# Moving the loads of v, k and q of chunks 2 to 5 into the first-layer stretch: forgetting attention and a GELU MLP on one core

## The chip, the cores and the metric

The kernel runs on one core of a Trainium2 chip. The metric is the device time of one execution in microseconds. The times shown are of three runs of the kernel before the change; a fourth execution was taken by the hardware profiler, and every row of the trace is from that one. Engines are named as in the profile: PE is TensorE (PEld its weight loads), DVE is VectorE, ACT is ScalarE, POOL is GpSimd, SP is SyncE. L208 is line 208 of the kernel.

## The reference

Attention with a forget gate for 8 batches of 8 heads, 576 tokens and head size 64, and behind it an MLP with GELU (tanh form) on all 4608 tokens, 512 to 2048 to 512 columns. All in float32.

```python
scores = scale * np.matmul(q, k.transpose(0, 1, 3, 2))
log_f = np.log(np.clip(f, 0.0001, 1.0))
cum = np.cumsum(log_f, axis=-1)
decay = cum[:, :, :, None] - cum[:, :, None, :]
scores = np.where(causal, -1000000000.0, scores + decay)
attn = softmax(scores)            # exp of scores less the row's maximum, over their sum + 1e-9
x = np.matmul(attn, v)            # then (B, S, H, D), as 4608 rows of 512
h = x @ w_in
g = 0.5 * h * (1.0 + np.tanh(c * (h + 0.044715 * h * h * h)))
out = g @ w_out
```

## The kernel before

**Tiling.** Attention works in quads: four heads of one batch, so two quads to a batch and 16 quads (0 to 15) in all. The MLP works in nine chunks of 512 tokens. The two run interleaved: while TensorE works on the first layer of chunk c (from d_model to d_ff, L395 and, by a scheme with seven products for eight, L520 and L468), and then on its second layer (L600), attention of the following quads is worked in between. A step of the program is one chunk; it has two stretches, the *first-layer stretch* and, after it, the *attention stretch*, in which the scores, masks and products of two quads alternate with pieces of the second layer.

**The order of the work** is written out by hand. Tables of words (`FRONT`, `SECOND`, `STEADY`, `FLUSH`, `LAST`) are run from left to right. A word names an operation and its arguments, and each engine gets its instructions in the order in which the words issue them. `FRONT` fills the machine, `SECOND` is run for chunk 2, `STEADY` for chunks 3, 4 and 5, `FLUSH` for chunk 6 and `LAST` for chunk 7. In a step for chunk c, a word on a quad has 2c added to its first number, and a word on a chunk or batch has c added; words on quads past 15 are dropped. So `LK.6` in chunk 3 loads k of quad 12, and `LB.2.4` in chunk 3 loads part 4 of batch 5.

**Words that matter here.**

- `LK.i`, `LQ.i` (`load_one`, L208) load k or q of quad i into one of two buffers, `k_c` or `q_c`. The load turns float32 into bfloat16 and is issued on GpSimd's queue, so it stands in order with GpSimd's other work.
- `TK.i`, `TQ.i` (`transpose_words`, L214) transpose such a buffer on VectorE into `kT` or `qT`. They wait for the load; the next load of the same buffer (two quads on) waits for them.
- `LB.b.t` (`load_v`, L185) loads rows 128t to 128t + 127 of all heads of v of batch b into one of two buffers `v_nat`, on SyncE's queue. Five such loads make a batch, the last with 64 rows. On the same queue, in order, go the stores of the output from `o_st` (L625), each of which waits for VectorE to write `o_st`.
- `VW.i` (`make_vw`, L231) multiplies v of a quad by its weights, on GpSimd, into `vw`. It is the reader of `v_nat`. In the step of chunk c, `VW.3` reads the batch loaded one step earlier and `VW.4` the one loaded in the same step.
- `S.i.r` (L277 and L285) are the scores of quad i in three rounds on TensorE with the exponential on ScalarE, `M.i.r` (L291) their causal masks on GpSimd, `D.i` and `V.i.x` (L347) the products with the weights and with v on TensorE, closed on VectorE (L366 to L379).
- `I`, `i`, `Q`, `E` are pieces of the first layer, `F` and `f` pieces of the second (L600), `G` the sums on VectorE between them (L578 to L584), `T` and `UW` other sums on VectorE.

**Buffers.** `k_c`, `q_c`, `kT`, `qT`, `v_nat`, `vw` and `pt` have two copies each, `o_st` three. In the step of chunk c, TensorE scores quads 2c + 3 and 2c + 4; the transposes of both stand in the first-layer stretch. The kernel before loads quad 2c + 5 in that stretch, and quad 2c + 6 in the attention stretch, one whole first-layer stretch ahead of its transposes in the next step.

Of the kernel before, what the change touches and what calls it, by code (L numbers as in the profile page):

```python
# [16 lines left out]
def kernel(  # L17
# [12 lines left out]
    B, H, S, D = q.shape  # L30
# [55 lines left out]
    """  # L86

    SECOND = """
        Y F.-1.99 T.0.1 T.0.2 T.0.3 T.0.4 I.0.0 E.0.2.2 I.0.1 TK.3 E.0.2.2 LK.5 TQ.3 LQ.5 TQ.4 I.0.2 LB.2.4 E.0.2.2 I.0.3 E.0.2.1 TK.4 LB.2.2 G.0 VW.3
        I.0.6 I.0.7 G.1.1.2 X LB.2.3 F.0.13 S.3.0 LB.2.0 LB.2.1 M.3.0 f.0.9 UW.0.1 D.2 f.0.9 S.3.1 LQ.6 M.3.1 V.2.0 f.0.12 S.3.2 M.3.2 LK.6 CL.3 V.2.1  # L90
        VW.4 f.0.14 S.4.0 UW.0.2 M.4.0 D.3 f.0.10 V.3.0 UW.0.4 CL.4 UW.0.3 S.4.1 f.0.13 M.4.1 V.3.1 S.4.2 F.0.9 M.4.2 F.0.2 F.0.1
    """

    STEADY = """
        Q.0.2 Y T.0.1 T.0.2 F.-1.2 Q.0.2 i.0.2.4 T.0.4 i.0.2.4 T.0.3 Q.0.2 TQ.3 Q.0.2 F.-1.6 i.0.3.4 Q.0.2 Q.0.2 TK.3 i.0.3.4 Q.0.2 TK.4 TQ.4 LB.2.2
        LQ.5 LB.2.3 F.-1.99 I.0.6 i.0.7 LK.5 G.0 S.3.0 X LB.2.4 G.1.1.2 LB.2.0 LB.2.1 f.0.16 M.3.0 D.2 VW.3 f.0.12 S.3.1 LQ.6 M.3.1 V.2.0 f.0.13 S.3.2
        M.3.2 CL.3 LK.6 V.2.1 VW.4 f.0.15 S.4.0 D.3 f.0.10 V.3.0 M.4.0 CL.4 S.4.1 f.0.14 M.4.1 V.3.1 S.4.2 F.0.12 M.4.2
    """

    FLUSH = """  # L100
# [758 lines left out]
```

## Time and profile before

| | us |
|---|---|
| median of 3 runs | 327.96 |
| the runs | 327.79, 327.96, 330.09 |
| the profiled execution | 329.55 |
| its span | 326.2 |
| granted TensorE clock in it | 0.999 |
| PE, DVE, ACT, POOL busy | 311.6, 242.7, 212.9, 106.7 |

In the rows of the trace, a line such as `166.36 0.41 PE L347 MATMUL po<-pt,vw ... x5` is start, duration, engine, line, operation, what is written from what, shapes, and how many instructions are merged in it; in brackets stands how long the engine was idle before it and what ended that. A row of a DMA queue gives its packets, their megabytes, and the time that they took as a share of 16 DMA engines in that window. A row of a DMA issue gives the count, the KB of each and the median time from issue to landing. In the list of waits a row gives who waited for whom, the sum in us, the times, and the longest.

Loads and stores of the whole program: 32 loads of k and q with 288 KB each, 40 loads of v from SyncE, 35 stores of 256 KB from `o_st`. The DMA queues are q0 (issued by GpSimd, 15.99 MB), q1 (issued by SyncE, 16.60 MB), and q8 and q14 (instructions, 0.67 and 0.07 MB).

### The profile page before, as it was taken

Reading aid. Unit: us, or ns where it says so; the run is one execution under the profiler, and the core shown is the slowest. Engines: PE = TensorE matmul, PEld = TensorE weight load, DVE = VectorE, ACT = ScalarE, POOL = GpSimd, SP = SyncE. Lnnn points to the kernel's source line nnn. Section 1 sums busy time; section 2 is a strip of 40 time slices with the busy share of each in tenths; the row PEclk is TensorE's granted clock in tenths of the full one; section 3 lists DMA queues with packets and bytes.
Section 4 is the critical chain, followed back from the end, with each engine's and each line's share of the span. In section 5 each row is a group of like instructions: output and inputs, shape, how many; then the busy total and the mean of one; then the engine's idle time right before and its main releaser. Section 6 shows DMA issues by size and latency. Waiting matters only on the chain.

```text
span 326.2 us, 11823 instructions
## 1 busy us (share of the span) xinstructions
PE 311.6 (96%) x5342; PEld 221.7 (68%) x5342; DVE 242.7 (74%) x374; ACT 212.9 (65%) x242; POOL 106.7 (33%) x145
## 2 busy tenths in 40 slices
PE   0899999999999999999989999999999999999996
PEld 0556844454677567776768876767776786788785
DVE  4665208898989978879876997699884866497574
ACT  4486567785856877778657875967677743846510
POOL 8868416343111406400841056204610150000000
PEclk9999999999999999999999999999999999999999
DMA  7999999686023954268333743184001012010202
GB/s 130 232 146 163 196 247 220 141 163 125 31 43 97 224 107 83 63 113 168 75 72 51 182 100 65 43 179 112 26 32 65 4 38 66 4 54 8 98 32 97
DMA packets 47490, 33.41 MB, mean 102 GB/s; under 512 B 29776, under 2 KB 42192, under 8 KB 47440
## 3 DMA queue, kind: packets, MB, share of 16 engines
q0 software_dynamic: 9632, 15.99, 29.3%
q1 hardware_dynamic: 37664, 16.60, 18.7%
q8 instruction: 41, 0.67, 0.8%
q14 instruction: 9, 0.07, 0.1%
q10 hardware_dynamic: 144, 0.07, 0.1%
HBM read 36.85 MB, written 9.44 MB: 142 GB/s over the span
## 4 chain that ended last, share of the span: by engine, by line
PE 81%; DMA 6%; POOL 4%; DVE 4%; ACT 3%; issue 2%; POOLq 0%; DVEq 0%
PE ps_w L600 29%; PE ps_h L395 17%; PE po L347 9%; PE ps_q L520 8%; PE ps_s L277 8%; DMA w_out_sb<-in_moe_w_out_dram 4%; PE ps_u L468 4%; PE pso L667 4%; DMA q_c<-in_q_dram 2%; ACT pt L285 1%; ACT gT L403 1%; POOL pt L291 1%; DVE gT L582 1%; POOL v_nat L185 1%; PE cum_ps L721 1%
## 5 line engine op out<-in xcount | busy, mean ns | idle before, releaser
L285 ACT ACTIVATE pt<-ps_s 128x1024 bf16<-128x1024 f32 (+2 forms) x100 | 93.9, 991 | 41.8 <-PE ps_s L277 38.5
L291 POOL TENSOR_SCALAR_AFFINE_SELECT pt<-pt 128x512 bf16<-128x512 bf16 (+3 forms) x65 | 39.6, 620 | 96.5 <-ACT pt L285 73.7
L395 PE MATMUL ps_h<-xT,w_in_sb 128*128 128x512 bf16 (+1 forms) x320 | 66.8, 358 | 0.3 <-ACT gT L403 0.2
L395 PEld LDWEIGHTS <-w_in_sb 128*128 128x128 bf16 x320 | 31.2, 98 | 26.6 <-issue 0.6
L600 PEld LDWEIGHTS <-gT 128*32 128x32 bf16 (+1 forms) x1216 | 44.2, 97 | 5.7 <-issue 2.4
L403 ACT ACTIVATE gT<-ps_h 128x1024 bf16<-128x1024 f32 x34 | 34.6, 1018 | 18.6 <-PE ps_h L395 18.3
L600 PE MATMUL ps_w<-w_out_sb,gT 128*32 128x256 bf16 (+1 forms) x1008 | 42.8, 273 | 0.0
L277 PE MATMUL ps_s<-qT,kT 32*128 32x64 bf16 (+5 forms) x896 | 36.4, 264 | 3.6 <-DVE qT L214 3.3
L600 PEld LDWEIGHTS <-gsum 128*32 128x32 bf16 (+1 forms) x948 | 35.4, 97 | 3.7 <-issue 1.3
L231 POOL TENSOR_TENSOR vw<-v_nat,wT 128x1280 bf16<-128x1280 f32 (+1 forms) x13 | 30.1, 2313 | 13.0 <-DMA v_nat<-in_v_dram 12.7
L536 DVE TENSOR_TENSOR usnap<-ps_q,usnap 128x1024 f32<-128x1024 f32 x15 | 17.9, 1222 | 19.4 <-PE ps_q L520 13.2
L277 PEld LDWEIGHTS <-kT 32*128 32x128 bf16 x896 | 16.5, 93 | 19.6 <-issue 10.2
L600 PE MATMUL ps_w<-usum,gsum 128*32 128x256 bf16 (+1 forms) x791 | 29.8, 273 | 0.0
L617 DVE COPY snap<-ps_w 128x512 f32<-128x512 f32 x32 | 21.8, 681 | 6.6 <-PE ps_w L600 6.5
L347 PE MATMUL po<-pt,vw 128*32 128x64 bf16 (+4 forms) x624 | 22.9, 278 | 1.3 <-issue 1.3
L379 DVE TENSOR_TENSOR xT<-po,rb 128x576 bf16<-128x576 f32 x26 | 19.6, 753 | 6.0 <-PE po L347 5.5
L531 ACT ACTIVATE gT<-usnap 128x1024 bf16<-128x1024 f32 x15 | 15.8, 1054 | 12.1 <-DVE usnap L536 11.8
L214 DVE STREAM_TRANSPOSE kT<-k_c 128x576 f32<-128x576 f32 x16 | 19.5, 1247 | 3.7 <-DMA k_c<-in_k_dram 3.7
L347 PEld LDWEIGHTS <-vw 128*32 128x32 bf16 x672 | 14.6, 97 | 11.2 <-issue 4.9
L214 DVE STREAM_TRANSPOSE qT<-q_c 128x576 f32<-128x576 f32 x16 | 19.8, 1247 | 2.7 <-DMA q_c<-in_q_dram 2.6
L208 POOL DMA_DIRECT2D k_c<-in_k_dram x16 | 9.0, 562 | 33.6 <-DVE kT L214 17.2
L520 PEld LDWEIGHTS <-w_in_sb 128*128 128x128 bf16 x160 | 15.6, 98 | 2.5 <-issue 0.4
(134 smaller groups left out, 481.1 us busy)
## 6 DMA issues: line engine op xcount, KB each, us to landing
out_dram<-o_st SPq DMA_DIRECT2D x35, 256.0 KB, 2.6
k_c<-in_k_dram POOLq DMA_DIRECT2D x16, 288.0 KB, 4.7
q_c<-in_q_dram POOLq DMA_DIRECT2D x16, 288.0 KB, 4.9
v_nat<-in_v_dram SPq DMA_DIRECT2D x16, 256.0 KB, 5.4
v_nat<-in_v_dram SPq DMA_DIRECT2D x20, 128.0 KB, 4.4
v_nat<-in_v_dram POOLq DMA_DIRECT2D x8, 256.0 KB, 7.9
w_in_sb<-in_moe_w_in_dram POOLq DMA_DIRECT2D x8, 256.0 KB, 7.2
w_out_sb<-in_moe_w_out_dram POOLq DMA_DIRECT2D x4, 512.0 KB, 10.8
```

The costliest lines, as they stand in the source:

```text
L214: return nc.vector.transpose(out=dst.rearrange("p s c -> p (s c)").bitcast(FP32) .rearrange("p (t a) -> p a t", a=S // 32), in_=src.rearra ...
L231: return eng.tensor_mul(vw[i % 2][:, t0:t1], vb[:, t0:t1, h0:h0 + 4, :], wT[:, i, t0:t1, :].unsqueeze(3).to_broadcast([128, t1 - t0, 4, D]))
L277: nc.tensor.matmul(tiles[h // 2][:, h % 2, c0:c0 + nq], key_columns(i, key, h, c), qq[32 * h:32 * h + 32, q0:q0 + nq, c], start=(c == 0 an ...
L285: nc.scalar.activation(p[:, 2 * g:2 * g + 2, off:off + n], t[:, :, 0:n], AF.Exp, scale=scale)
L291: nc.gpsimd.affine_select(out=x, in_=x, compare_op=ALU.is_ge, fill=0.0, base=0, pattern=pattern, channel_multiplier=-1)
L347: nc.tensor.matmul(po[r0:r0 + w.shape[-1], 448 + q0:448 + q0 + nq], w, p[:, h, col:col + nq], start=(key in (0, "low")), stop=(key in ("lo ...
L379: nc.vector.tensor_mul(xT[:, 2 * u + x, r0 + s0:r0 + s1], po, rbs[i, part])
L395: nc.tensor.matmul(ph[:, j, n * cols:(n + 1) * cols], w_in_sb[:, dt, 128 * ft:128 * ft + 128], xT[:, dt, h0:h0 + cols], start=(dt == 0 and ...
L403: nc.scalar.activation(gelus(c, 2 * pr, 2), ph, AF.Gelu_apprx_tanh)
L520: nc.tensor.matmul(ps[:, k, HC * n:HC * n + HC], w[:, d, 128 * n:128 * n + 128], x[:, d, :], start=(first and n == 0 and d == 0), stop=(d ...
L600: nc.tensor.matmul(ps[c0:c0 + width, n, cols[0]:cols[1]], x[:, j, 128 * n + c0:128 * n + c0 + width], w[:, j, cols[0]:cols[1]], start=(fir ...
L617: copy(kept[name], ps)
```

## The change

Only the tables `SECOND` and `STEADY` change; no operation is added or left out. The five loads of v, which stood late in the first-layer stretch and at the start of the attention stretch (`LB.2.2`, `LB.2.3`, `LB.2.4`, `LB.2.0`, `LB.2.1`), stand at the front and the middle of the first-layer stretch, in rising order. The loads of k and q of the even quads (`LQ.6`, `LK.6` in the attention stretch) are taken out there; in `STEADY` they stand as `LK.4`, `LQ.4` at the front of the next step, which is the same quad. The loads of the odd quads (`LK.5`, `LQ.5`) stand directly behind the transposes that free their buffers.

```diff
     SECOND = """
-        Y F.-1.99 T.0.1 T.0.2 T.0.3 T.0.4 I.0.0 E.0.2.2 I.0.1 TK.3 E.0.2.2 LK.5 TQ.3 LQ.5 TQ.4 I.0.2 LB.2.4 E.0.2.2 I.0.3 E.0.2.1 TK.4 LB.2.2 G.0 VW.3
-        I.0.6 I.0.7 G.1.1.2 X LB.2.3 F.0.13 S.3.0 LB.2.0 LB.2.1 M.3.0 f.0.9 UW.0.1 D.2 f.0.9 S.3.1 LQ.6 M.3.1 V.2.0 f.0.12 S.3.2 M.3.2 LK.6 CL.3 V.2.1
-        VW.4 f.0.14 S.4.0 UW.0.2 M.4.0 D.3 f.0.10 V.3.0 UW.0.4 CL.4 UW.0.3 S.4.1 f.0.13 M.4.1 V.3.1 S.4.2 F.0.9 M.4.2 F.0.2 F.0.1
+        Y F.-1.99 T.0.1 T.0.2 LB.2.0 T.0.3 T.0.4 LB.2.1 I.0.0 LB.2.2 E.0.2.2 I.0.1 LB.2.3 TK.3 LK.5 LB.2.4 E.0.2.2 TQ.3 LQ.5 TQ.4 I.0.2 E.0.2.2 I.0.3
+        E.0.2.1 TK.4 G.0 VW.3 I.0.6 I.0.7 G.1.1.2 X F.0.13 S.3.0 M.3.0 f.0.9 UW.0.1 D.2 f.0.9 S.3.1 M.3.1 V.2.0 f.0.12 S.3.2 M.3.2 CL.3 V.2.1 VW.4
+        f.0.14 S.4.0 UW.0.2 M.4.0 D.3 f.0.10 V.3.0 UW.0.4 CL.4 UW.0.3 S.4.1 f.0.13 M.4.1 V.3.1 S.4.2 F.0.9 M.4.2 F.0.2 F.0.1
     """
 
     STEADY = """
-        Q.0.2 Y T.0.1 T.0.2 F.-1.2 Q.0.2 i.0.2.4 T.0.4 i.0.2.4 T.0.3 Q.0.2 TQ.3 Q.0.2 F.-1.6 i.0.3.4 Q.0.2 Q.0.2 TK.3 i.0.3.4 Q.0.2 TK.4 TQ.4 LB.2.2
-        LQ.5 LB.2.3 F.-1.99 I.0.6 i.0.7 LK.5 G.0 S.3.0 X LB.2.4 G.1.1.2 LB.2.0 LB.2.1 f.0.16 M.3.0 D.2 VW.3 f.0.12 S.3.1 LQ.6 M.3.1 V.2.0 f.0.13 S.3.2
-        M.3.2 CL.3 LK.6 V.2.1 VW.4 f.0.15 S.4.0 D.3 f.0.10 V.3.0 M.4.0 CL.4 S.4.1 f.0.14 M.4.1 V.3.1 S.4.2 F.0.12 M.4.2
+        LK.4 LQ.4 Q.0.2 Y LB.2.0 T.0.1 T.0.2 LB.2.1 F.-1.2 Q.0.2 i.0.2.4 T.0.4 LB.2.2 i.0.2.4 T.0.3 Q.0.2 TQ.3 LQ.5 Q.0.2 F.-1.6 i.0.3.4 Q.0.2 Q.0.2
+        LB.2.3 TK.3 LB.2.4 LK.5 i.0.3.4 Q.0.2 TK.4 TQ.4 F.-1.99 I.0.6 i.0.7 G.0 S.3.0 X G.1.1.2 f.0.16 M.3.0 D.2 VW.3 f.0.12 S.3.1 M.3.1 V.2.0 f.0.13
+        S.3.2 M.3.2 CL.3 V.2.1 VW.4 f.0.15 S.4.0 D.3 f.0.10 V.3.0 M.4.0 CL.4 S.4.1 f.0.14 M.4.1 V.3.1 S.4.2 F.0.12 M.4.2
     """
```

In the built programs TensorE's, VectorE's and ScalarE's instructions stand in the same order. GpSimd's differ only in the three pairs of loads (k and q of quads 10, 12 and 14), which stand behind the last masks of a step instead of among the masks of its first quad. SyncE's differ in the place of the v loads among the stores: in chunk 2 they stand behind the same stores as before, in another order among themselves; in chunks 3 to 5 three of them stand one store earlier than the first did before, and the other two behind the next store.

## The prediction

> **What bounds the kernel now.** I read the page first: span, busy times, chain.
>
> ```profile
> span 326.2 us, 11823 instructions
> PE 311.6 (96%) x5342; PEld 221.7 (68%) x5342; DVE 242.7 (74%) x374; ACT 212.9 (65%) x242; POOL 106.7 (33%) x145
> PE 81%; DMA 6%; POOL 4%; DVE 4%; ACT 3%; issue 2%; POOLq 0%; DVEq 0%
> ```
>
> TensorE is busy 96% of the span and carries 81% of the chain of waits. So a moved load is worth something only where TensorE stands still because of it. The profiled execution took 329.55 us, 3.35 more than its span; the median of the runs shown is 327.96, 1.59 below it.
>
> Next I cut the span of chunks 3, 4 and 5 into their two stretches: first layer, then attention. A stretch begins at the first matmul of that part, by the timeline of TensorE. The busy times by windows say this (columns: stretch, length, busy time with count for PE, PEld, DVE, ACT, POOL, then granted clock, DMA share, GB/s):
>
> ```profile
> 134.00:150.55 16.55, 16.55 (x120) 11.59 (x121) 12.94 (x17) 13.05 (x14) 2.35 (x4) 1.00 0.53 99
> 150.55:168.82 18.27, 17.43 (x578) 13.00 (x578) 15.85 (x25) 12.07 (x13) 10.34 (x12) 1.00 0.50 102
> 168.82:185.46 16.64, 16.64 (x154) 14.73 (x154) 11.97 (x16) 13.05 (x14) 2.35 (x4) 1.00 0.48 101
> 185.46:203.24 17.78, 17.28 (x578) 12.85 (x578) 15.11 (x24) 12.07 (x13) 10.34 (x12) 1.00 0.49 103
> 203.24:219.79 16.55, 16.55 (x120) 11.59 (x122) 12.79 (x17) 13.05 (x14) 2.35 (x4) 1.00 0.48 101
> 219.79:236.76 16.97, 16.97 (x578) 12.83 (x578) 14.89 (x24) 12.07 (x13) 9.66 (x10) 1.00 0.30 74
> ```
>
> The first-layer stretches are full: TensorE is busy all 16.55 to 16.64 us. The attention stretches do the same 578 matmuls but differ: 18.27, 17.78 and 16.97 us. Chunk 5's is the fast one, and it is the one without a k and a q load, because quad 16 does not exist (POOL x10 instead of x12, DMA share 0.30 instead of 0.50). The before kernel thus holds a sample of what the changed attention stretch would be. The excess is 18.27 - 16.97 = 1.30 us in chunk 3 and 17.78 - 16.97 = 0.81 us in chunk 4.
>
> The waits of TensorE and its timeline show most of it:
>
> ```profile
> PE po L347 <- issue: 1.3, 2, 0.8
> ```
> ```profile
> 166.36 0.41 PE L347 MATMUL po<-pt,vw 128*32 128x512 bf16 x5
> 167.61 0.65 PE L347 MATMUL po<-pt,vw 128*32 128x64 bf16 x19 [0.84 <-issue]
> 198.12 0.73 PE L347 MATMUL po<-pt,vw 128*32 128x512 bf16 x13
> 199.35 0.43 PE L347 MATMUL po<-pt,vw 128*32 128x320 bf16 x11 [0.50 <-issue]
> ```
>
> One product of 24 matmuls stops after 5, another after 13, for 0.84 and 0.50 us, with nothing to wait for that the profile shows. What can stop an engine inside a product is the lack of instructions, so I asked for the DMA packets. In chunk 3, 160.0 to 165.2, then 165.2 to 166.3:
>
> ```profile
> q0 software_dynamic: 275, 0.57, 75.9%
> ```
> ```profile
> q8 instruction: 1, 0.02, 5.4%
> ```
>
> In chunk 4, 192.0 to 197.1, then 197.1 to 200.3:
>
> ```profile
> q0 software_dynamic: 141, 0.29, 37.2%
> q1 hardware_dynamic: 272, 0.26, 15.3%
> ```
> ```profile
> q8 instruction: 1, 0.02, 1.9%
> ```
>
> In chunk 5, 228.0 to 231.4, then 231.4 to 232.6:
>
> ```profile
> q1 hardware_dynamic: 272, 0.26, 23.5%
> q8 instruction: 1, 0.02, 1.8%
> ```
> ```profile
> q8 instruction: 1, 0.02, 5.7%
> ```
>
> Queue q8 brings TensorE's instructions. In chunk 5 one of its packets starts in each stretch of about 3.4 us, with a store on q1 in flight. In chunks 3 and 4 there is none for more than 5 us while the k and q loads (q0, the GpSimd queue) are in flight, and TensorE stops 1.6 to 1.8 us after the late packet could start at the earliest (166.36 + 0.41 = 166.77 against 165.2; 198.85 against 197.1). I read this as refills held up by the k and q loads. In the first layer TensorE uses 120 to 154 matmuls in 16.6 us instead of 578 in 17, so a refill there has several times longer before it is missed.
>
> **The change part by part.** In all parts instructions and bytes are the same; only places change. Rows of GpSimd, VectorE and SyncE in chunk 3 carry this part:
>
> ```profile
> 136.10 1.23 POOL L291 TENSOR_SCALAR_AFFINE_SELECT pt<-pt 128x512 bf16<-128x512 bf16 x2 [2.14 <-ACT pt L285]
> 140.85 0.59 POOL L208 DMA_DIRECT2D q_c<-in_q_dram  x1 [3.53 <-DVE qT L214]
> 147.17 0.53 POOL L208 DMA_DIRECT2D k_c<-in_k_dram  x1 [5.73 <-DVE kT L214]
> 156.22 2.33 POOL L231 TENSOR_TENSOR vw<-v_nat,wT 128x1280 bf16<-128x1280 f32 x1
> 158.50 0.59 POOL L208 DMA_DIRECT2D q_c<-in_q_dram  x1
> 159.11 0.65 POOL L291 TENSOR_SCALAR_AFFINE_SELECT pt<-pt 128x512 bf16<-128x512 bf16 x1
> 160.80 1.23 POOL L291 TENSOR_SCALAR_AFFINE_SELECT pt<-pt 128x512 bf16<-128x512 bf16 x2 [1.04 <-ACT pt L285]
> 161.98 0.55 POOL L208 DMA_DIRECT2D k_c<-in_k_dram  x1
> 162.55 2.35 POOL L231 TENSOR_TENSOR vw<-v_nat,wT 128x1280 bf16<-128x1280 f32 x1
> ```
> ```profile
> 145.62 2.33 DVE L214 STREAM_TRANSPOSE kT<-k_c 128x576 f32<-128x576 f32 x2
> 147.79 1.24 DVE L214 STREAM_TRANSPOSE qT<-q_c 128x576 f32<-128x576 f32 x1
> ```
> ```profile
> 134.62 7.58 SPq L625 DMA_DIRECT2D out_dram<-o_st  x2
> 142.29 1.36 SPq L185 DMA_DIRECT2D v_nat<-in_v_dram  x2
> 150.01 2.05 SPq L185 DMA_DIRECT2D v_nat<-in_v_dram  x3
> ```
>
> Attention stretch, k and q loads of even quads (three pairs leave it, from chunks 2, 3 and 4). GpSimd's masks move up by 0.59 us at most (the one at 159.11 stands right behind a load); the next pair waits 1.04 us for ScalarE anyway, so that is worth nothing on TensorE. What is gained is the refill: I take the chunk 5 stretch for chunks 3 and 4, 1.30 + 0.81 = 2.11 us. Lower bound: the two gaps alone, 0.84 + 0.50 = 1.34. Upper bound: chunk 2 loses a pair too, and shows no gap; if it hides as much as chunk 3 has beside its gap (1.30 - 0.84 = 0.46), the gain is 2.57.
>
> First-layer stretch, the same three pairs. They stand behind the last two masks of the chunk before, so in chunk 3 they issue at 136.10 + 1.23 = 137.33 and 0.55 later. GpSimd then idles 3.53 and 5.73 us before its next two loads, which keep their places: issue costs nothing. Who waits is VectorE: the second kT transpose at about 146.8 (half of the two from 145.62) and qT at 147.79. The trace's busiest load time was in chunk 2, loads issued from 109.9 to 112.1, beside the worst landing of any q load:
>
> ```profile
> v_nat<-in_v_dram SPq DMA_DIRECT2D x3, 256.0 KB, 6.9
> k_c<-in_k_dram POOLq DMA_DIRECT2D x1, 288.0 KB, 5.4
> q_c<-in_q_dram POOLq DMA_DIRECT2D x1, 288.0 KB, 6.4
> ```
> ```profile
> DMA to landing us min/median/max: 3.8/4.9/12.6
> ```
>
> With 5.4 and 6.4 us, k lands at 142.7 and q at 144.3: 4.1 and 3.5 us early. With 12.6 both come late, k by 3.1 and q by 2.7 us. I take the first, since those loads stood between v loads on a full DMA, as these will; cost zero, at the other end 3.1 us in each of three chunks.
>
> v loads. In chunks 3 to 5 three of five follow the store at 134.62 and two the store before 142.29, instead of two at 142.29 and three at 150.01. Their buffer has been free since the chunk before (its last reader is such a product as the one at 156.22). Their reader in the same chunk is the product at 162.55: with 6.9 us of landing from 144, they are there by 151. Behind them on SyncE stand only stores. In chunk 2 they come behind the same two stores as before and only change order. Cost zero; that cover would be gone only with landings over 18 us.
>
> TensorE's refills in the first layer now meet more loads. By the fast stretch's 578 matmuls in 16.97 us and the first layer's 120 to 154 in 16.6, the use there is about four times slower, so the cover of a refill grows in the same measure; a delay of 2 us as in attention stays hidden. Bounds: 0 and, if one refill per chunk were missed as in chunk 3, 0.84 x 3 = 2.5 us. I take 0, as the three first-layer stretches show no gap with DMA shares of 0.48 to 0.53.
>
> Two rules of the Trainium skill speak against the gain. "Runtime: NRT & Kernel Launch", section Instruction fetch mechanics, says that the sequencer streams 16 KiB blocks on its own while it executes the current one, and that a boundary is mostly hidden. The block size agrees with the 0.02 MB of each q8 packet; that it is hidden does not fit the two gaps behind late packets. "DMA: Bandwidth & Descriptors", section Queues, rings and completion order, says that each engine takes turns between queues packet by packet, so that a load could hold a refill for one packet only; here none starts for 5 us. By either rule the sum would be 0 instead of -2.11.
>
> Sum: -2.11 (from -2.57 to -1.34). On the profiled execution 329.55 becomes 327.44; on the median 327.96 becomes 325.85. I forecast 325.9.
>
> **The rivals.** A: the gaps have another cause and stay. A refill may be late for itself, and the loads beside it chance; then the time is 327.96. Against it: both gaps follow a late packet, and the stretch without k and q has neither. It is also what the two rules above would make of it. Chance 0.09.
>
> B: the gaps belong to the profiled execution, 1.59 us slower than the median. If the timed runs refill in time, there is nothing to gain: 327.96. For it: the difference has the size of the gain. Against it: the loads stand in the same place in every run. Chance 0.09.
>
> C, slower: the moved k and q land late. VectorE then stands at the second kT transpose, with qT, the copy of the store, the sums for the second layer and the denominators queued behind it, and TensorE waits for these. It decides once a landing takes longer than 146.8 - 137.33 = 9.5 us. At 12.6 us it costs 3.1 us in each of three chunks, 9.3 in all; with the 2.11 gained, 327.96 + 9.3 - 2.1 = 335.2. For it: all four k and q loads and all v loads now share one first layer; v alone has five loads there. Against it: 5.4 and 6.4 us on a full DMA. Chance 0.12.
>
> D: more than 1% is gained, as the loads also slow VectorE in attention (15.85 us of work in chunk 3, 14.89 in chunk 5). TensorE does not wait for VectorE there, so 0.05; about 324.5.
>
> **How the numbers follow.** Forecast 0.65, and the rest as above. The range begins at 327.96 - 2.57 = 325.4, less 0.2 for the distance of the two nearest runs (327.79 and 327.96): 325.2. It ends with A and B at 327.96 plus twice that: 328.3. C and D, 0.17 together, are left out. A measurement of this kernel tells about 1% (3.3 us) from no change. Faster by more than that is D: 0.05. Slower by more is C: 0.12. The forecast, A and B lie within it: 0.83.
>
> **What would show it.** Right: attention stretches of chunks 3 and 4 near 17.0 us; no "issue" gap in a product; q8 packets there 3.4 us apart; q0 silent in attention. First-layer stretches stay at 16.6, with a DMA share well above 0.53. Wrong: an idle time of VectorE before kT or qT that ends with a k or q load (C); a gap of TensorE left in attention with q0 silent (A); a gap of TensorE by "issue" in a first layer (its refills missed after all).

## The result, and the profile after

The changed kernel took 325.14 us (median of 22 runs, 323.55 to 327.70), the kernel before, measured beside it, 327.23 us (22 runs, 325.44 to 330.09). The ratio is 0.9943 with a 95% interval of 0.9923 to 0.9962: 1.9 us less, between 1.2 and 2.5. That is clear of zero and below 1%. Ratios here and below leave out a few slow executions, the slowest of them 457.91 and 365.22 us at granted clocks of 0.66 and 0.86.

The busy times by windows of the changed kernel, cut like those of before (first-layer and attention stretch of chunks 3, 4 and 5; stretch, length, busy time with count for PE, PEld, DVE, ACT, POOL, granted clock, DMA share, GB/s):

```profile
135.44:151.99 16.55, 16.55 (x121) 11.59 (x122) 12.84 (x17) 13.05 (x14) 3.37 (x6) 1.00 0.88 177
151.99:168.96 16.97, 16.97 (x578) 12.87 (x578) 14.89 (x24) 12.07 (x13) 9.64 (x10) 1.00 0.11 35
168.96:185.59 16.63, 16.63 (x152) 14.71 (x153) 12.84 (x17) 13.04 (x14) 3.36 (x6) 1.00 0.85 176
185.59:202.57 16.98, 16.98 (x578) 12.87 (x578) 14.84 (x24) 12.07 (x13) 9.63 (x10) 1.00 0.10 34
202.57:219.12 16.55, 16.55 (x122) 11.59 (x120) 12.78 (x17) 13.04 (x14) 3.36 (x6) 1.00 0.87 176
219.12:236.10 16.98, 16.98 (x578) 12.79 (x578) 14.88 (x24) 12.07 (x13) 9.64 (x10) 1.00 0.11 36
```

All three attention stretches now last 16.97 to 16.98 us, the length that chunk 5 had before. The first-layer stretches kept theirs, although the DMA share there went from about 0.5 to 0.85 to 0.88. In the DMA packets of chunk 3's attention stretch (152 to 169) q0 is all but silent, and five packets of TensorE's instructions come, 3.4 to 4.3 us apart:

```profile
q1 hardware_dynamic: 527, 0.51, 8.9%
q8 instruction: 5, 0.08, 2.1%
q0 software_dynamic: 2, 0.00, 0.0%
```

The moved loads land in time. The issues from 138 to 149 with their time to landing, and the transposes on VectorE that wait for them:

```profile
k_c<-in_k_dram POOLq DMA_DIRECT2D x2, 288.0 KB, 5.0
q_c<-in_q_dram POOLq DMA_DIRECT2D x2, 288.0 KB, 6.5
```
```profile
147.06 2.33 DVE L214 STREAM_TRANSPOSE kT<-k_c 128x576 f32<-128x576 f32 x2
149.23 1.24 DVE L214 STREAM_TRANSPOSE qT<-q_c 128x576 f32<-128x576 f32 x1
```

No idle time stands before them: no bracket follows the rows. One "issue" gap is left among TensorE's waits, and it is not in these chunks but in the fill, at L419, about 32 us from the start:

```profile
PE ps_h L419 <- issue: 2.0, 1, 2.0
```

Chunk 2's attention stretch begins at 119.8 us in this execution and at 118.4 in that of the kernel before, so the spans differ by only 0.7 us (325.5 against 326.2). From there to the end it is 207.8 us before and 205.7 after.

### The profile page after: what moved, and what is told of

The parts are those of the page before. It is cut to its first block, busy times and chain, and to the rows that moved or that the text cites. A ratio compares the mean times of both kernels' runs of the same rounds, so it can differ in the third digit from the quotient of the medians.

```text
span 325.5 us, 11826 instructions
## 1 busy us (share of the span) xinstructions
PE 312.0 (96%) x5342; PEld 222.2 (68%) x5342; DVE 241.6 (74%) x374; ACT 212.7 (65%) x242; POOL 107.2 (33%) x145
## 4 chain that ended last, share of the span: by engine, by line
PE 91%; ACT 3%; DVE 2%; DMA 2%; issue 1%; POOL 0%; DVEq 0%; POOLq 0%
PE ps_w L600 30%; PE ps_h L395 19%; PE ps_s L277 9%; PE po L347 9%; PE ps_q L520 8%; PE ps_h L419 5%; PE pso L667 4%; PE ps_u L468 4%; DMA q_c<-in_q_dram 2%; PE po_m L333 1%; ACT pt L285 1%; PE cum_ps L721 1%; ACT gT L403 1%; DVE xT L379 1%; PE idle_ps L256 0%
## 5 line engine op out<-in xcount | busy, mean ns | idle before, releaser
L291 POOL TENSOR_SCALAR_AFFINE_SELECT pt<-pt 128x512 bf16<-128x512 bf16 (+3 forms) x65 | 40.8, 637 | 97.6 <-ACT pt L285 74.8
L395 PEld LDWEIGHTS <-w_in_sb 128*128 128x128 bf16 x320 | 31.2, 98 | 26.7 <-issue 0.6
L419 PE MATMUL ps_h<-xT,w_in_sb 128*128 128x256 bf16 x128 | 16.3, 291 | 2.0 <-issue 2.0
```

The source lines that it names most:

```text
L291: nc.gpsimd.affine_select(out=x, in_=x, compare_op=ALU.is_ge, fill=0.0, base=0, pattern=pattern, channel_multiplier=-1)
L395: nc.tensor.matmul(ph[:, j, n * cols:(n + 1) * cols], w_in_sb[:, dt, 128 * ft:128 * ft + 128], xT[:, dt, h0:h0 + cols], start=(dt == 0 and ...
L419: nc.tensor.matmul(ph[:, j // 2, QA * (j % 2):QA * (j % 2) + QA], w_in_sb[:, dt, 128 * ft:128 * ft + 128], xT[:, dt, n0:n0 + QA], start=(d ...
```

## The experiments

Below, "excess" is the length of the attention stretches of chunks 3, 4 and 5 above 16.97 us, read from the busy times by windows. It was 1.30 + 0.81 + 0.00 = 2.11 us before, and 0.02 after. The times of whole runs scatter by 3 us and more between executions of the same kernel, so that six or twelve of them resolve about 1 us. The excess is of one execution, but it holds nearly all by which the traces differ behind the fill: from the start of chunk 2's attention stretch to that of chunk 3's it is 32.15 to 32.17 us in every kernel but the two with wide matmuls, and from the end of chunk 5's to the last matmul 86.5 us in all. (Behind the last matmul, the first execution with only k and q moved and the one with v loaded again took 1.7 and 1.5 us longer than the others.) Both measures are given.

**One part alone.** Two kernels take the change apart: only k and q moved, only v moved.

```diff
 # only k and q: the kernel before, in SECOND and STEADY (there LK.6 stood behind CL.3)
-... S.3.1 LQ.6 M.3.1 ... M.3.2 LK.6 CL.3 ...
+... S.3.1 M.3.1 ... M.3.2 CL.3 ...
 # and at the front of STEADY
-        Q.0.2 Y T.0.1 T.0.2 F.-1.2 ...
+        LK.4 LQ.4 Q.0.2 Y T.0.1 T.0.2 F.-1.2 ...
```

> The kernel before with only the three pairs of k and q loads (quads 10, 12, 14) moved to the front of the next step; the v loads stay where they were. Theory (the k and q loads in flight hold up TensorE's instruction packets): the whole gain, 2.1 us below the kernel before (ratio about 0.994); attention stretches of chunks 3 and 4 at 17.0 us, no issue gap in a product. Rival (v loads, or DMA traffic as a whole, hold the packets): the v loads that still run into the attention stretch keep a part of the loss; less than half of the gain, ratio 0.997 or above, and gaps of 0.2 us or more remain in chunk 3 or 4.

```diff
 # only v: the changed kernel, with LQ.6 and LK.6 back in SECOND and STEADY
-        LK.4 LQ.4 Q.0.2 Y LB.2.0 T.0.1 ...
+        Q.0.2 Y LB.2.0 T.0.1 ...
-... S.3.1 M.3.1 ... S.3.2 M.3.2 CL.3 ...
+... S.3.1 LQ.6 M.3.1 ... S.3.2 M.3.2 CL.3 LK.6 ...
 # (in SECOND: M.3.2 LK.6 CL.3)
```

> The changed kernel with the three pairs of k and q loads put back into the attention stretch; only the v loads are moved. Theory: no gain, ratio 0.999 to 1.001; issue gaps of about 0.5 to 0.9 us in the products of chunks 3 and 4, stretches of 17.8 to 18.3 us. Rival (v loads or traffic as a whole): at least half of the gain, ratio 0.997 or below, gaps shorter than 0.3 us.

With only k and q moved the ratio to the kernel before was 0.9935 (0.990 to 0.997), the excess 0.56 + 0.20 + 0.00 = 0.76 us. With only v moved it was 0.9933 (0.9901 to 0.9964), the excess 0.26 + 1.41 + 0.00 = 1.67 us. So neither expectation held as a whole: by the trace most of the loss goes with k and q but a third stays, and by the runs the two halves could not be told apart. The timeline of TensorE with only v moved shows a product stopped after 13 of 24 matmuls, the one that stopped there in the kernel before:

```profile
195.60 0.73 PE L347 MATMUL po<-pt,vw 128*32 128x512 bf16 x13
197.44 0.43 PE L347 MATMUL po<-pt,vw 128*32 128x320 bf16 x11 [1.11 <-issue]
```

With only k and q moved TensorE stops elsewhere, in the second layer near the start of chunk 3's attention stretch (which begins at 148.91), where v loads are in flight. Up to 151.5 no packet of q8 starts; in the changed kernel the first comes 1.2 us into the stretch. The gap, and the packets from 148.91 to 151.5:

```profile
153.72 0.29 PE L600 MATMUL ps_w<-w_out_sb,gT 128*32 128x256 bf16 x3 [0.28 <-issue]
```
```profile
q1 hardware_dynamic: 1303, 0.52, 75.5%
q0 software_dynamic: 16, 0.02, 3.7%
```

**Loads that nobody reads.** The changed kernel, with k and q loaded once more in attention:

```diff
-... S.3.1 M.3.1 V.2.0 f.0.13 S.3.2 M.3.2 CL.3 V.2.1 ...
+... S.3.1 LQ.4 M.3.1 V.2.0 f.0.13 S.3.2 M.3.2 CL.3 LK.4 V.2.1 ...
```

> The changed kernel, and in the attention stretches of chunks 3, 4 and 5 the k and q of the quad just transposed are loaded once more, at the places where the pairs stood before; nobody reads them. Theory: the loss comes back, and in chunk 5 too, which never had it: stretches of 17.5 to 18.3 us in all three, issue gaps within products in at least two of them, 2 to 3.5 us above the changed kernel. Rival (the loss lay in the order of the loads that are waited for, not in the traffic): no gap, as nobody waits for these loads, and the time of the changed kernel within 0.5 us.

Ratio 0.9954 (0.9926 to 0.9983), the highest of the four kernels measured together, though still below the kernel before; excess 0.30 + 1.37 + 0.01 = 1.68 us. In the trace the loss comes back although nothing waits for these loads, and the gap stands after the same 13 matmuls:

```profile
196.49 0.73 PE L347 MATMUL po<-pt,vw 128*32 128x512 bf16 x13
198.27 0.43 PE L347 MATMUL po<-pt,vw 128*32 128x320 bf16 x11 [1.05 <-issue]
```

But chunk 5 stayed at 16.98, with k and q in flight. The expectation failed there: such loads in the stretch are not enough. In the packets of its stretch (223.6 to 235.7) three of q8 came, none of them late enough to be missed:

```profile
q0 software_dynamic: 288, 0.59, 32.7%
q1 hardware_dynamic: 272, 0.26, 6.6%
q8 instruction: 3, 0.05, 1.9%
```

The one that came while k and q were under way started in a lull between the two. From 230.25 to 230.85, and from there to 231.05:

```profile
q0 software_dynamic: 8, 0.01, 7.1%
```
```profile
q8 instruction: 1, 0.02, 41.2%
```

**Small loads at the same places**, 64 of the 1152 columns of each row:

```diff
+    def load_some(src, dst, i):
+        b, h0 = i // QPB, 4 * (i % QPB)
+        return nc.gpsimd.dma_start(
+            out=dst[i % 2].rearrange("p a d -> p (a d)")[:, 0:D],
+            in_=src[b, h0:h0 + 4].rearrange("h (p a) d -> (h p) (a d)", p=32)[:, 0:D])
...
-... S.3.1 M.3.1 V.2.0 f.0.13 S.3.2 M.3.2 CL.3 V.2.1 ...
+... S.3.1 SQ.4 M.3.1 V.2.0 f.0.13 S.3.2 M.3.2 CL.3 SK.4 V.2.1 ...
```

> The changed kernel with small loads at the places where the k and q loads stood in attention in chunks 3, 4 and 5: the same 128 rows, but 64 of 1152 columns, read by nobody. GpSimd's queue is occupied as before, the traffic is a twentieth. Theory (traffic of k and q in flight holds the packets): no gap, stretches at 17.0 us, time of the changed kernel within 0.5 us. Rival (the issue on GpSimd among the masks, not the traffic): stretches of 17.5 us or more and 1 us or more lost.

Ratio 0.9918 (0.9886 to 0.995), stretches 16.97, 16.98 and 16.98. GpSimd issues as many instructions among the masks as before (x12), and nothing is lost:

```profile
149.09:166.06 16.97, 16.97 (x578) 12.88 (x578) 15.11 (x24) 12.07 (x13) 10.32 (x12) 1.00 0.15 38
```

So it is the bytes in flight, not the issue on GpSimd's queue.

**The same with v**, from SyncE's queue:

```diff
-... f.0.12 S.3.1 M.3.1 V.2.0 ...
+... f.0.12 S.3.1 LB.1.0 LB.1.1 LB.1.2 LB.1.3 LB.1.4 M.3.1 V.2.0 ...
```

> The changed kernel, and in the attention stretches of chunks 3, 4 and 5 the five v loads of the batch just read are issued once more on SyncE behind the second round of scores of the first quad; nobody reads them. They bring 1.1 MB, about as much DMA time as a pair of k and q. Theory (it is the loads of GpSimd's queue that hold the packets): no gap, stretches at 17.0 us, time of the changed kernel within 0.5 us. Rival (any traffic of that size holds them): gaps and 2 to 3.5 us, as with k and q loaded again.

The expectation failed in the trace. The runs were the fastest of the four kernels measured together (0.9914, 0.9884 to 0.9945), but the trace has gaps of 0.63 us in chunk 5 and 0.29 us behind chunk 4's stretch: stretches 16.98, 17.12 and 17.89 (excess 1.08 us), and the first layer of chunk 5 at 17.00 instead of 16.55. TensorE's timeline, and the packets from 228.5 to 230.0, where a packet of q8 at last starts:

```profile
230.19 1.48 PE L600 MATMUL ps_w<-usum,gsum 128*32 128x256 bf16 x45
232.30 0.51 PE L600 MATMUL ps_w<-usum,gsum 128*32 128x256 bf16 x11 [0.63 <-issue]
```
```profile
q1 hardware_dynamic: 1388, 0.35, 118.3%
q8 instruction: 1, 0.02, 5.3%
```

From 224.7 to 229.5 there was none. So v loads can hold TensorE's packets too.

**Fewer instructions.** The second-layer matmuls of attention 128 columns wide instead of four times 32, in the kernel before and in the changed one (in `STEADY`, and alike in `SECOND`):

```diff
-... f.0.16 M.3.0 D.2 VW.3 f.0.12 S.3.1 ... f.0.13 ... f.0.15 ... f.0.10 ... f.0.14 ...
+... F.0.16 M.3.0 D.2 VW.3 F.0.12 S.3.1 ... F.0.13 ... F.0.15 ... F.0.10 ... F.0.14 ...
```

> The kernel before with the second-layer matmuls of the attention stretches of chunks 2 to 5 issued 128 columns wide instead of four times 32: the same products, about a quarter of the instructions in them. The loads stay as before. Theory (the gaps are late instruction packets, missed only because attention uses instructions fast): packets come about half as often, no issue gap, although k and q are in flight; stretches of chunks 3, 4 and 5 equal within 0.2 us. Rival (the loads slow TensorE otherwise, by its reads or writes): chunks 3 and 4 stay 0.5 to 1.3 us longer than chunk 5.

> The changed kernel with the second-layer matmuls of the attention stretches of chunks 2 to 5 issued 128 columns wide. Theory: with rare packets the place of the loads does not matter; equal to the kernel before with the same wide matmuls, within 0.5 us. Rival: still 1.5 us or more faster than that. What wide matmuls do to the time by themselves is open: from 2 us slower, if the changes of shape between them and the attention matmuls cost, to 1 us faster.

The three stretches of the kernel before, wide:

```profile
149.60:167.34 17.74, 17.74 (x338) 11.89 (x338) 14.97 (x24) 12.07 (x13) 10.32 (x12) 1.00 0.50 101
183.97:201.70 17.73, 17.73 (x338) 11.88 (x338) 14.92 (x24) 12.07 (x13) 10.32 (x12) 1.00 0.51 104
218.25:235.99 17.74, 17.74 (x338) 11.89 (x338) 14.80 (x24) 12.07 (x13) 9.64 (x10) 1.00 0.27 70
```

The loads are where they were (DMA share 0.50, 0.51, 0.27), and the stretches are equal within 0.01 us, with no gap. In the first of them two packets of q8 come instead of five:

```profile
q8 instruction: 2, 0.03, 0.7%
```

Over the whole program q8 brings 34 packets instead of 41 for 8827 matmuls and weight loads instead of 10684, about 260 to a packet both times: it follows TensorE's instructions.

The changed kernel, wide, has 17.73, 17.74 and 17.74. The ratios to the kernel before are 0.9985 (0.9956 to 1.0014) and 0.9998 (0.9972 to 1.0024): with about half as many packets in attention the place of the loads is worth nothing that the runs show. Nor is it that no packet came late: in the kernel before, wide, the third packet of chunk 4's stretch starts 15.2 us into it and the first of chunk 5's 3.7 us, in the changed kernel, wide, 14.0 and 2.3 us. These delays left no gap. The wide matmuls themselves cost 0.77 us in each stretch (17.74 against 16.97), so they are no better way.

**A late landing**, the price of rival C:

```diff
-        LK.4 LQ.4 Q.0.2 Y LB.2.0 ...
+        Q.0.2 Y LB.2.0 ...
-        LB.2.3 TK.3 LB.2.4 LK.5 i.0.3.4 Q.0.2 TK.4 TQ.4 ...
+        LB.2.3 TK.3 LB.2.4 LK.5 LK.4 LQ.4 i.0.3.4 Q.0.2 TK.4 TQ.4 ...
```

> The changed kernel with the k and q loads of quads 10, 12, 14 put behind the k load of the odd quad, the last load of GpSimd's queue in the first-layer stretch, so that they issue some 10 us later and land after VectorE comes to their transposes. It prices the slower rival of the prediction. Theory (a landing after the transposes costs TensorE what VectorE stands, less a little slack): VectorE idles 4 to 7 us before the second kT transpose in each of three chunks, TensorE loses 3 to 6 us in each, 9 to 18 us in all. Rival (VectorE has enough slack there): less than 1 us in a chunk, 3 us in all.

356.47 us, a ratio of 1.0862 (1.082 to 1.0904). VectorE stood as long as expected, 5.8 us, but TensorE lost more than the 3 to 6 us: 10.1 us in chunk 3, and 31.0 us in the three attention stretches instead of 9 to 18. VectorE's idle time, TensorE's two waits, and the granted clock behind them (window, then PE, PEld, DVE, ACT, POOL, clock):

```profile
151.36 1.26 DVE L214 STREAM_TRANSPOSE kT<-k_c 128x576 f32<-128x576 f32 x1 [5.79 <-DMA k_c<-in_k_dram]
```
```profile
154.60 1.49 PE L600 MATMUL ps_w<-w_out_sb,gT 128*32 128x256 bf16 x48 [2.11 <-DVE o_st L622]
162.55 1.53 PE L347 MATMUL po<-pt,vw 128*32 128x512 bf16 x24 [5.88 <-DVE den L366]
```
```profile
149.25:176.27 27.02, 19.02 (x578) 14.26 (x578) 20.70 (x28) 12.07 (x13) 10.08 (x10) 0.87 0.19 44
163.00:168.00 5.00, 5.00 (x124) 3.72 (x120) 3.48 (x6) 0.72 (x1) 0.00 (x0) 0.67 0.17 56
```

TensorE waits 2.11 us for the copy that frees a bank and 5.88 us for the denominators, both queued on VectorE behind the transposes. That is 8.0 of the 10.1 us. The other 2 us are longer matmuls: the mean clock of 0.67 is one of 0.50 up to 166.25, granted from 159.4 on, in the middle of the wait, and 3.7 us of it fall on matmuls.

**Again, measured together:** the kernel before, the changed one and the two halves.

> The kernel before once more, for a second profiled execution. Excess means the length of the attention stretches of chunks 3, 4 and 5 above 16.97 us, summed; it was 2.11 us. Theory now (any DMA traffic in attention can hold TensorE's instruction packets, and the gaps fall where a packet comes due while loads are in flight): they come again, an excess of 1.2 to 3 us. Rival (they belonged to that one execution): below 0.5 us. Time: equal to the kernel before.

> The changed kernel once more. Theory: excess below 0.1 us again, as only stores are in flight in attention. Rival (the clean stretches were one execution's luck): 0.5 us or more. Time: 1.5 to 2.5 us below the kernel before, in the same call as the two kernels that do one part alone.

> Only the k and q loads moved, once more; its excess was 0.56 + 0.20 + 0.00 = 0.76 us. Theory now: the v loads at the start of attention hold packets too, so an excess of 0.3 to 1.2 us again, and less gain than the whole change. Rival (k and q alone matter): below 0.2 us.

> Only the v loads moved, once more; its excess was 0.26 + 1.41 + 0.00 = 1.67 us, though its timed runs were as fast as those of the other half. Theory now: the k and q loads hold packets here, excess 0.8 to 2.2 us, and the timed gain is the smaller of the two halves, 0.0 to 1.3 us. Rival (the v loads carry the gain): excess below 0.5 us and a timed gain of 1.5 us or more.

| | ratio to before | excess, chunks 3, 4, 5 | excess in the first execution |
|---|---|---|---|
| before, again | 0.9998 (0.9965 to 1.003) | 1.01 + 0.60 + 0.11 = 1.72 | 2.11 |
| changed, again | 0.9887 (0.9844 to 0.993) | 0.00 + 0.01 + 0.00 = 0.01 | 0.02 |
| only k and q | 0.9955 (0.9922 to 0.9989) | 0.53 + 0.15 + 0.00 = 0.68 | 0.76 |
| only v | 0.9964 (0.9935 to 0.9994) | 0.97 + 1.13 + 0.00 = 2.10 | 1.67 |

The loss is no accident of one execution. In the kernel before, a product of chunk 3 stops again after 5 of its 24 matmuls, as in the first execution, only shorter (0.58 us instead of 0.84):

```profile
165.34 0.41 PE L347 MATMUL po<-pt,vw 128*32 128x512 bf16 x5
166.33 0.65 PE L347 MATMUL po<-pt,vw 128*32 128x64 bf16 x19 [0.58 <-issue]
```

Moving only k and q leaves 0.7 us, of which 0.5 us is the first part of chunk 3's stretch (5.01 us instead of 4.48), where v loads are in flight. Moving only v leaves the whole excess. Its timed gain of 0.4% (0.1 to 0.7%, and 0.7% the first time) has no counterpart in the two traces: from the start of chunk 2's attention stretch to the end they take 207.4 and 207.8 us, the kernel before 207.8 and 207.4. So this gain lies ahead of that stretch or outside the span, or comes of the scatter, and it stays open; k and q loaded again raise the same question. That the loss goes mostly with k and q rests on the traces, not on the times. The changed kernel gained more here than the first time and than expected (0.9887, some 3.7 us, against 0.9943; the intervals overlap by a little); its excess says 0.5 to 0.6%, and I take the comparison with 22 runs on each side.

**Packet by packet.** Over all these traces the gap follows the packet. In each of the eleven "issue" gaps of 0.25 us or more in these attention stretches a packet of q8 started 2.2 to 2.7 us before TensorE went on. In chunk 4's stretch the fourth packet starts 9.6 to 9.8 us after the stretch began in the changed kernel (both executions) and with small loads: excess 0.01 us. It starts at 10.6 with v loaded again and with only k and q moved, second execution (0.15), at 11.0 in the first execution of that (0.20), at 11.5 and 11.7 in the kernel before (0.60 and 0.81), and at 12.0 to 12.3 with only v moved and with k and q loaded again (1.13 to 1.41). Most of the first 1 us of delay is covered; beyond that the loss grows with the delay.

## Why the prediction was right, point by point

- **Forecast and term.** 325.9 us against 325.14, and a gain of 2.11 against 1.9 (1.2 to 2.5) by the runs and 2.09 by the excess of the first executions (2.11 - 0.02); 1.71 in the second (1.72 - 0.01). Chunk 5's stretch as a sample of the others was the right one: 16.97 to 16.98 us in all three. A little luck is in it: the kernel before, again, had 17.08 us there. The upper bound let chunk 2 hide 0.46 us; from its attention stretch to chunk 3's it is 32.15 us before and 32.16 after, so nothing was hidden. That the timed gain is all of this term is not shown, since the runs with only v moved gained without it.
- **The gaps are late instruction packets.** Held. They come where the loads' bytes are in flight and nobody waits for them (k and q loaded again), not with the same issues of few bytes, and not when TensorE needs half as many packets. Rival A falls with the changed kernel, twice: the same order of TensorE's instructions, no such loads in flight, packets in time and no gap in attention. The wide kernels show that the same loads cost nothing where instructions are used more slowly. The gaps also stop a product at the same matmul, after 5 in chunk 3 and after 13 in chunk 4, in both executions of the kernel before and wherever only v was moved or k and q were loaded again and a product stopped there. A place in the instruction stream does that; a busy moment of the DMA alone would not.
- **"Held up by the k and q loads".** This step was too narrow. The v loads hold packets as well: 0.7 us of excess is left when only k and q move, and v loaded again brings gaps of its own. In the kernel before itself 0.25 us of chunk 3's 1.30 stand in the first part of the stretch (4.73 us instead of 4.48), before its k and q loads are issued. Nor does every such load hold one: in chunk 5 of the kernel before, v loads fill the first 4.48 us just so (DMA share 0.87), and the first packet still starts 1.1 us in, as in the changed kernel. What decides this is not shown. The prediction gave the moved v loads no part in the gain. The sum came out since both were moved, and that much is luck.
- **Rival B**, the gaps as an accident of the profiled execution: the second one has 1.72 us of excess.
- **Rival C**, late landings: did not occur. The loads took 5.0 and 6.5 us (median of two) against the 5.4 and 6.4 assumed. Its price was too low, since it let TensorE lose only what VectorE stands; with VectorE idle 5.8 us TensorE lost 10.1. The landing of 12.6 us was also no near row: it is from the fill, where the DMA share is 0.98 to 1.08 in the first 60 us. That, and not chunk 2 with 0.87, is the trace's busiest load time.
- **First-layer refills**: cost zero, as taken, at DMA shares of 0.85 to 0.88. A first layer did lose 0.45 us where v was loaded again (a gap of 0.29 us at its start, behind a late packet), so the cover there is not unlimited.
- **The two rules of the Trainium skill** named in the prediction ("Runtime: NRT & Kernel Launch", Instruction fetch mechanics; "DMA: Bandwidth & Descriptors", Queues, rings and completion order) gave no gain. The measurement decides: most blocks are hidden here too (three of the 41 packets of the kernel before stand ahead of an "issue" gap of more than 0.4 us), but not every one beside such loads. Why a packet of one queue waits so long beside the others is not shown by any run here.

## What to carry to other kernels

Idle time of TensorE by "issue" within an accumulation, at the same matmul in several executions, pointed here to its instruction stream; look for the packets of its instruction queue and for what else is in flight then. Big loads belong where TensorE uses few instructions per microsecond, as long as they land before their reader; a reader on a busy engine that came to them early cost more than its own wait, 10.1 us against 5.8. A stretch of the same program that happens to lack the suspected cost was a good estimate of the gain.

## What the runs showed that I had not expected

The fill is what scatters most, though its table (`FRONT`) is the same in all these kernels. The attention stretch of chunk 2 began between 116.3 us (v loaded again) and 119.8 us (the changed kernel, first execution). In that execution a packet of TensorE's instructions was late in the fill too. TensorE's timeline there, and the DMA packets from 30 to 33 us, which take all the time of the DMA engines:

```profile
30.57 1.26 PE L419 MATMUL ps_h<-xT,w_in_sb 128*128 128x256 bf16 x10
33.83 1.56 PE L419 MATMUL ps_h<-xT,w_in_sb 128*128 128x256 bf16 x9 [2.00 <-issue]
```
```profile
q0 software_dynamic: 441, 0.59, 107.4%
q8 instruction: 1, 0.02, 2.0%
```

This one gap of 2.00 us is as large as the whole gain, and behind it the granted clock was 0.50 for 3.4 us. In the second execution of the changed kernel chunk 2's attention stretch began 3.3 us earlier, at 116.5 us. In the kernel before the gap was 0.44 us in its first execution, and in the second execution of the changed kernel there was none of that size. An effect of half a per cent was to be read here from the stretches, not from the span.
